# Sparse attention and a feed-forward layer in one kernel: seven instead of ten pairs of attention tiles ahead of the FFN, and the first group's sixteen f-tiles in one row

## The chip, the core and the metric

The kernel runs on one core of one Trainium2 chip. The metric is the device time of one execution in microseconds. Every duration and time of day below is in microseconds unless marked ns; times of day count from the start of the profiled span.

## The reference

Attention over 8 batches, 8 heads, 576 positions and 64 columns a head. Heads 0 to 3 have a local mask (a query sees the 32 positions that end at it), heads 4 to 7 a strided one (a query sees the earlier positions with the same remainder modulo 32). The result, 4608 tokens by 512, goes through a feed-forward layer of width 2048.

```
rel = pos[:, None] - pos[None, :]
mask_local = (rel >= 0) & (rel < 32)
mask_strided = (rel >= 0) & (pos[None, :] % 32 == pos[:, None] % 32)
scores = where(mask, scale * q @ k.T, -1e9)        # per batch and head
attn = exp(scores - max); attn /= sum(attn) + 1e-9
x = (attn @ v), heads side by side                 # 4608 x 512
h = x @ w_in                                       # 512 x 2048
g = h * sigmoid(1.702 * h)
out = g @ w_out                                    # 2048 x 512
```

## The kernel before, in words

**Attention.** Only the blocks that the masks leave are computed. A unit of work is a pair: two neighbouring tiles of queries for all four heads of one kind. A local tile has 96 queries and 128 keys. A strided tile holds the positions of 6 or 5 remainders, 18 positions each, so 108 or 90 queries and as many keys. A batch has three strided pairs (of 108, 90 and 90 rows) and three local pairs. There are 48 pairs. Of each, TensorE makes the scores (`s`, or `u` for odd pairs in the pipeline), VectorE the negated maximum (`nmax`), ScalarE eight exponentials with their sums, VectorE the reciprocals, GpSimd the multiplication by them (`pr`). Then `pr` is transposed into `pt_l` or `pt_s`, TensorE multiplies by v (`a`), ScalarE rounds the result to the upper part of x (`xhl`, `xhs`), and VectorE subtracts to get the lower part (`xll`, `xls`).

**Feed-forward.** The tokens are worked in twelve groups of 384, the width in sixteen f-tiles of 128. Every operand of a product is split in an upper and a lower part, and three products stand for one: `ffn1` (line 447) issues 12 products of 128 x 384 into `h`, `act` (line 461) makes tanh on ScalarE, `g` on VectorE, `gh` on ScalarE and `gl` on VectorE, and `ffn2` (line 480) issues 9 products of 128 x 512 into the three output banks `o` of the group. The main loop (line 599) runs over a list `steps` of (group, f-tile). Turn s issues `ffn1` of step s, `act` of step s - 1, work on pairs, and `ffn2` of step s - 2 (`LAG`).

**Weights.** w_in and w_out come as pairs of 32-bit words, 1 MB an f-tile, into tiles `raw` (`load_w`, line 336). `weights` (line 401) is a generator. Each of its beats, a unit, is one large ScalarE operation, followed one beat later by its VectorE operation: scale, then low with a join on VectorE (both on `raw`), then split (`w<-raw` on ScalarE, `w<-raw,w` on VectorE). So an f-tile takes three units, and split of f-tile f is unit 3f + 4. `raw` and the finished weights share 16 tiles, so the last f-tile is only loaded when the one ahead of it is finished. `weigh(n)` (line 440) runs the generator up to n units; one of a turn's units stands inside `act`, between tanh and `gh`.

**The order of the work.** `InOrder` (line 98) keeps TensorE's instructions in program order throughout, and those of VectorE, ScalarE, GpSimd and the DMA queue on SyncE as long as weights are still to be made (line 600). So the queues of these engines in that stretch are read off the program. Before the main loop stands a pipeline over the first `n0` pairs (lines 550 to 578). There the mask is added by a product on TensorE, and `pr` is transposed by TensorE (`turn_pr`, banks `t`). The later pairs stand in the main loop: `windows` lists those that belong to each next group, `due` gives the turn at which VectorE transposes a pair, `turn` the same the other way round, and `begins` the turn at which its scores are made. Values follow one turn after the transposes. The pair's exponentials are spread over the turns between (line 627).

In before, `n0` is 10: groups 0 and 1 have all their pairs in the pipeline. `spans` (line 527) puts the first eight f-tiles of group 0, then group 1 whole, then the second half of group 0. Weights are made at three units a turn for eight turns and at one and a half a turn after that (line 619). Group 0's first half is kept in SBUF (`halves`, line 501) and added at the end (line 510).

Of the kernel before, what the change touches and what calls it, by code (L numbers as in the profile page):

```python
# [18 lines left out]
P = 128  # L19
# [23 lines left out]
SOON = 11  # L43
LAG = 2
RAWB = 4
NH = NF // 2
WEIGHED = 7


def _pairs():  # L50

    def strided(b):
        return [("s", b, c) for c in range(0, len(RES), U)]

    def local(j):
        n = G // QL
        return [("l", i // NL, i % NL) for i in range(j * n, (j + 1) * n, U)]

    def weave(a, b):
        return [u for i in range(max(len(a), len(b))) for u in a[i : i + 1] + b[i : i + 1]]

    first = {}
    for b in range(B):
        first.setdefault(b * S // G, []).extend(strided(b))
    ahead = local(0) + first[0]
    windows = [weave(first.get(j + 1, []), local(j + 1)) for j in range(NG - 1)] + [[]]
    ahead += windows[0]
    windows[0] = []  # L70
    return ahead + [u for w in windows for u in w], windows, len(ahead)


# [1 line left out]
def attn_ffn(ctx, tc, qk, vs, w_in, w_out, masks, ident, out):  # L75
# [48 lines left out]
    def load_qk(p):  # L124
        if p < len(pairs) and p not in qks:
            qks[p] = st4([P, 2, 2, U, P], F32, f"qk_{p}")
            for g in (slice(0, 1), slice(1, 2)) if p == 0 else (slice(0, 2),):
                sync.dma_start(out=qks[p][:, :, g], in_=qk[p][:, :, g])
# [63 lines left out]
    def maxima(p):  # L192


        nq, nk, mask = geom(p)
        sps, pr, n = banks.pop(p), prs[p % AHEAD], mask.shape[1]
        nmax = nmaxs[p] = small.tile([P, HU], F32, tag="nmax", name=f"nmax_{p}")
        if p < n0:
            for j in range(2):
                vector.tensor_reduce(  # L200
                    out=nmax[:nq, j * 2 * U : (j + 1) * 2 * U],
                    in_=sps[j][:nq, : 2 * U * nk].rearrange("p (h n) -> p h n", n=nk),
                    axis=AX.X, op=ALU.max, negate=True,
                )
            vector.tensor_scalar_mul(out=nmax[:nq], in0=nmax[:nq], scalar1=SCALE)
            exps[p] = [
                (sps[i // (2 * U)][:nq, i % (2 * U) * nk : (i % (2 * U) + 1) * nk], SCALE)
                for i in range(HU)
            ]
            return  # L210
        for j in range(2):
            o = pr[:nq, j * 2 * U : (j + 1) * 2 * U, :nk]
            if n == 2:
                o = o.rearrange("p (g u) n -> p g (u n)", g=2)
            vector.scalar_tensor_tensor(
                out=o, in0=sps[j][:nq, : 2 * U * nk].rearrange("p (a n) -> p a n", a=n),
                scalar=SCALE, in1=mask, op0=ALU.mult, op1=ALU.add,
            )
        vector.tensor_reduce(
            out=nmax[:nq], in_=pr[:nq, :, :nk], axis=AX.X, op=ALU.max, negate=True  # L220
        )
        exps[p] = [(pr[:nq, i, :nk], 1.0) for i in range(HU)]
# [159 lines left out]
    def split_w(f):  # L382

        part = w_tile([P, 2, 2, DM], F32R, f"w_{f}")
        wih[f], wil[f] = (part[:, 0, i].rearrange("p (c n) -> p c n", c=NC) for i in range(2))
        woh[f], wol[f] = (part[:, 1, i] for i in range(2))
        vs = [(part[:, m, 0], part[:, m, 1], v) for m, v in words.pop(f)]

        def high():
            for hi, _, v in vs:  # L390
                scalar.copy(out=hi, in_=v)

        def low():
            for hi, lo, v in vs:
                vector.tensor_tensor(out=lo, in0=v, in1=hi.bitcast(F32), op=ALU.subtract)
            if f + RAWB < NF - 1:
                load_w(f + RAWB)

        return high, low
# [40 lines left out]
    def weigh(n):  # L440

        while made[0] < n and next(wgen, 0) is None:
            made[0] += 1
# [31 lines left out]

    outs = {}

    halves = {}

    def ffn2(j, f, i, parts):  # L480


        first = (0, NH) if j == 0 else (0,)
        last = (NH - 1, NF - 1) if j == 0 else (NF - 1,)
        if f in first and 0 in parts:
            outs[j, i] = bank(f"o_{j}_{i}")
        ps = outs[j, i]
        gh, gl = gs[j, f]
        tok = slice(i * P, (i + 1) * P)
        ws = ((gh, woh), (gh, wol), (gl, woh))  # L490
        for n in parts:
            g, w = ws[n]
            matmul(
                ps, lhsT=g[:, tok], rhs=w[f],
                start=(f in first and n == 0), stop=(f in last and n == 2),
            )
        if f not in last or 2 not in parts:
            return
        del outs[j, i]
        if f < NF - 1:  # L500
            o = halves[i] = const.tile([P, DM], F32, name=f"half_{i}")
            if i == 1:
                vector.tensor_scalar_mul(out=o, in0=ps, scalar1=0.5)
            else:
                scalar.mul(out=o, in_=ps, mul=0.5)
            return
        make = st4 if j == NG - 1 and i == 2 else st2
        o = make([P, DM], F32, f"out_{j}_{i}")
        if j == 0:
            vector.scalar_tensor_tensor(  # L510
                out=o, in0=ps, scalar=0.5, in1=halves[i], op0=ALU.mult, op1=ALU.add
            )
        elif i == 1:
            scalar.mul(out=o, in_=ps, mul=0.5)
        else:
            vector.tensor_scalar_mul(out=o, in0=ps, scalar1=0.5)
        r = j * G + i * P
        sync.dma_start(out=out[r : r + P, :], in_=o)
        if i == NT - 1:
            del xs["l", j], xs["s", j]  # L520
# [3 lines left out]
            next(gen, None)  # L524


    spans = [(0, 0, NH), (1, 0, NF), (0, NH, NF)] + [(j, 0, NF) for j in range(2, NG)]
    steps = [(j, f) for j, f0, f1 in spans for f in range(f0, f1)]
    load_qk(1)
    load_v(0)  # L530
    ident_sb = const.tile([P, P], F32, name="ident_sb")
# [8 lines left out]
    def scaled(p):  # L540
        run(halfway.pop(p))

    def late_part(p):
        run(valued.pop(p))
# [5 lines left out]
    for i in range(n0):  # L550
        if i + 1 < n0:
            scores(i + 1)
            load_qk(i + 3)
        if i >= 1:
            scaled(i - 1)
        if i >= 2:
            fetch_pt(i - 2)
        if i >= 3:
            late_part(i - 3)
        if i + 1 < n0:  # L560
            maxima(i + 1)
        halfway[i] = softmax(i)
        run(halfway[i], 4)
        if i >= 2:
            value_products(i - 2)
            load_v(i)
            run(valued[i - 2], 1)
        if i % 2 and i // 2 + 1 < RAWB:
            load_w(i // 2 + 1)
        weigh(i and i + 1)  # L570
        if i == n0 - 2:
            turn_pr(i - 1)
            ffn1(*steps[0], (0, 1))
        elif i == n0 - 1:
            ffn1(*steps[0], (2, 3))
            turn_pr(i - 1)
        elif i >= 1:
            turn_pr(i - 1)


    at = {}
    for n, (j, f) in enumerate(steps):
        at.setdefault(j, n)
    due = {}
    p = n0
    for j, w in enumerate(windows):
        if not w:
            continue
        end = at[j + 1]
        begin = end - NH + 1 if j == 1 else at[j]  # L590
        for i in range(len(w)):
            due[begin + i * (end - 1 - begin) // len(w)] = p
            p += 1

    late, turn = None, {p: s for s, p in due.items()}
    begins = {}
    for p in range(n0, len(pairs)):
        begins[max(turn.get(p - AHEAD, -1) + 1, turn[p] - SOON)] = p
    for s in range(len(steps) + LAG):
        strict[0] = made[0] < 3 * NF + 3  # L600
        cur = steps[s] if s < len(steps) else None
# [1 line left out]
        p, q, r = due.get(s), due.get(s - 1), begins.get(s)  # L603
        if cur:
            if s == 1:
                scaled(n0 - 1)
                fetch_pt(n0 - 2)
                late_part(n0 - 3)
            if s == 2:
                fetch_pt(n0 - 1)  # L610
                late_part(n0 - 2)
            if s > 0:
                ffn1(*cur, range(NC))
            if s in (1, 2):
                value_products(n0 - 3 + s)
            if s == 1:
                turn_pr(n0 - 1)
        if 0 < s <= len(steps):
            goal = WEIGHED + min(3 * (s + 1), 3 * NH + (s + 1 - NH) * 3 // 2)
            act(*steps[s - 1], lambda: weigh(min(made[0] + 1, goal)))  # L620
            if s in (1, 2):
                run(valued[n0 - 3 + s], 1)
            weigh(goal)
            if s == 2:
                late_part(n0 - 1)
        if late is not None:
            run(late[0], -(-4 // (late[1] - s)) if late[1] > s else HU)
        if p is not None:
# [96 lines left out]
```

## Time and profile before

| | |
|---|---|
| median of 3 runs | 940.06 us (939.3 to 940.83) |
| profiled execution | 941.84 us, its span 940.1 us, mean granted TensorE clock 0.998 |
| TensorE, VectorE, ScalarE, GpSimd busy | 98%, 55%, 43%, 9% of the span |
| `o` products (1728) | 44% of the chain that ended last |
| `h` products (2304) | 43% of that chain |
| bytes moved | 65.10 MB, mean 69 GB/s |

The page gives busy time by engine, the span in 40 slices, the chain of work that ended last and groups of instructions. A row of a timeline has the start, the time covered, the engine, the line (all instructions are recorded at line 108, the helper that issues them), the operation, output and inputs by name, the shapes and the count; in brackets stands the idle time before it and what ended it. A row of the chain has the start, the time and what it was. A row of windows has the stretch, then busy time of each engine, the granted clock, the share of the DMA engines and GB/s.

### The profile page before, as it was taken

To read this page: it belongs to the slowest core of one execution; us is meant where nothing else is said; L and a number is where in the kernel's file an instruction comes from. 1 tells how busy PE (TensorE), PEld (TensorE's weight loads), DVE (VectorE), ACT (ScalarE), POOL (GpSimd) and SP (SyncE) were. 2 spreads that over 40 slices of the span, in tenths; PEclk is the share of its full clock that TensorE was granted. 3 is DMA by queue.
4 is the path that set the end of the run, shared out by engine and by line. 5 is a ranking of instruction groups with operands and counts; after the bars stand their busy time and mean duration, and the time that the engine had idled before them with its cause. 6 is when DMAs were issued, how large, how long until landed. Compare 5 with 4: busy or idle time off the path is not lost.

```text
span 940.1 us, 14682 instructions
## 1 busy us (share of the span) xinstructions
PE 924.2 (98%) x5668; PEld 815.1 (87%) x5668; DVE 520.3 (55%) x999; ACT 408.0 (43%) x1289; POOL 85.7 (9%) x56
## 2 busy tenths in 40 slices
PE   7799999999999999999999999999999999999998
PEld 5589888888888888888888888898888888888997
DVE  4886564676666554626756665544756665422322
ACT  6997563434344443325343443333344444222221
POOL 3310000011001100101010100000010101000000
PEclk9999999999999999999999999999999999999999
DMA  8894020222121111103212121102211210000000
GB/s 269 307 336 172 1 90 29 73 68 68 48 77 59 54 36 66 35 1 102 60 42 81 54 69 45 36 22 68 65 37 56 80 46 12 34 1 1 34 1 33
DMA packets 24373, 65.10 MB, mean 69 GB/s; under 512 B 2672, under 2 KB 3440, under 8 KB 24304
## 3 DMA queue, kind: packets, MB, share of 16 engines
q1 hardware_dynamic: 24304, 64.17, 20.4%
q8 instruction: 44, 0.72, 0.3%
q14 instruction: 25, 0.20, 0.1%
HBM read 54.72 MB, written 9.44 MB: 68 GB/s over the span
## 4 chain that ended last, share of the span: by engine, by line
PE 95%; DVE 2%; DMA 1%; ACT 1%; issue 0%; POOL 0%; SPq 0%; ACTq 0%; POOLq 0%
PE o L108 44%; PE h L108 43%; PE s L108 4%; PE a L108 4%; DMA qk<-qk 1%; ACT pr L108 1%; PE u L108 1%; DVE nmax L108 0%; PE t L108 0%; DVE w L108 0%; DVE raw L108 0%; POOL pr L108 0%; DVE pt_l L108 0%; ACT raw L108 0%; SPq L108 0%
## 5 line engine op out<-in xcount | busy, mean ns | idle before, releaser
L108 PE MATMUL o<-w,gh 128*128 128x512 f32 x1152 | 307.8, 399 | 0.0
L108 PEld LDWEIGHTS o<-w,gh 128*128 128x128 f32 x1152 | 210.9, 188 | 40.0
L108 PE MATMUL h<-xhl,w 128*128 128x384 f32 x768 | 231.3, 342 | 0.4 <-DVE w L108 0.4
L108 PE MATMUL h<-xhs,w 128*128 128x384 f32 x768 | 226.3, 335 | 0.0
L108 DVE SCALAR_TENSOR_TENSOR g<-g,h 128x384 f32<-128x384 f32 x192 | 106.4, 554 | 195.8 <-ACT g L108 194.8
L108 ACT ACTIVATE g<-h 128x384 f32<-128x384 f32 x192 | 93.6, 488 | 246.2 <-PE h L108 178.6
L108 PE MATMUL o<-w,gl 128*128 128x512 f32 x576 | 169.4, 395 | 0.0
L108 DVE TENSOR_TENSOR gl<-g,gh 128x384 fp32r<-128x384 f32 x192 | 126.2, 657 | 73.5 <-ACT gh L108 72.3
L108 ACT ACTIVATE pr<-pr,nmax 96x128 f32<-96x128 f32 (+2 forms) x304 | 114.2, 378 | 113.1 <-DVE nmax L108 109.6
L108 ACT CAST gh<-g 128x384 fp32r<-128x384 f32 x192 | 99.0, 516 | 130.2 <-DVE g L108 129.9
L108 PEld LDWEIGHTS h<-xhl,w 128*128 128x128 f32 x768 | 141.5, 188 | 9.4 <-DVE w L108 0.7
L108 POOL TENSOR_TENSOR pr<-pr,rinv 96x1024 f32<-96x1024 f32 (+2 forms) x48 | 82.1, 1710 | 708.0 <-DVE rinv L108 631.5
L108 PEld LDWEIGHTS h<-xhs,w 128*128 128x128 f32 x768 | 141.5, 188 | 0.1
L108 PEld LDWEIGHTS o<-w,gl 128*128 128x128 f32 x576 | 108.2, 188 | 26.0
L108 PE MATMUL h<-xll,w 128*128 128x384 f32 x384 | 129.7, 338 | 0.0
L108 PE MATMUL h<-xls,w 128*128 128x384 f32 x384 | 128.3, 334 | 0.0
L108 PEld LDWEIGHTS h<-xll,w 128*128 128x128 f32 x384 | 72.1, 188 | 8.5
L108 PEld LDWEIGHTS h<-xls,w 128*128 128x128 f32 x384 | 72.1, 188 | 0.0
L108 DVE TENSOR_SCALAR rinv<-ssum 96x8 f32<-96x8 f32 (+2 forms) x48 | 8.0, 167 | 93.9 <-ACT pr L108 93.8
L108 ACT ACTIVATION_READ_ACCUMULATOR pr<-pr,nmax 96x1 f32 (+2 forms) x304 | 57.1, 188 | 0.0
L108 DVE STREAM_TRANSPOSE pt_l<-pr 32x256 f32<-32x256 f32 x120 | 52.1, 434 | 3.7 <-POOL pr L108 2.3
L108 PE MATMUL s<-qk 64*96 64x128 f32 (+2 forms) x688 | 46.2, 274 | 1.7 <-DMA qk<-qk 1.7
(52 smaller groups left out, 543.2 us busy)
## 6 DMA issues: line engine op xcount, KB each, us to landing
qk<-qk SPq DMA_DIRECT2D x47, 512.0 KB, 4.2
v<-vs SPq DMA_DIRECT2D x48, 256.0 KB, 2.9
out<-out SPq DMA_DIRECT2D x36, 256.0 KB, 2.5
raw<-w_in SPq DMA_DIRECT2D x16, 512.0 KB, 5.4
raw<-w_out SPq DMA_DIRECT2D x16, 512.0 KB, 6.2
qk<-qk SPq DMA_DIRECT2D x2, 256.0 KB, 4.0
masks_sb<-masks SPq DMA_DIRECT2D x1, 128.0 KB, 2.1
ident_sb<-ident SPq DMA_DIRECT2D x1, 64.0 KB, 5.5
```

What stands on the lines that cost most here:

```text
L108: ins = call(*args, **kw)
```

## The change

The pipeline ahead of the FFN holds seven pairs: the five of group 0 and group 1's two local ones. Group 1's three strided pairs become a window of group 0, due at turns 6, 9 and 12, with their scores at turns 3, 7 and 10. The steps run group by group, sixteen f-tiles each, and the half sums go. The goal of units at turn s is 6 + 3(s + 1) up to turn 2 and 8 + 3(s + 1) after. In the pipeline, w_1 is loaded one iteration sooner and the loads of w_2 to w_4 are placed by hand; part of the first products moves past the end of the pipeline. Group 2's two local pairs, the first of the later windows, become due at turns 18 and 24 in place of 25 and 28. The negated maximum of pair 0 is scaled by halves, and the last output tile is evicted by ScalarE and VectorE together.

```diff
-NH = NF // 2
-WEIGHED = 7
+NEARLY = 5
+WEIGHED = 6, 8
...
-    ahead += windows[0]
-    windows[0] = []
+    ahead += windows[0][1::2]
+    del windows[0][1::2]
...
             for j in range(2):
+                heads = slice(j * 2 * U, (j + 1) * 2 * U)
...
-            vector.tensor_scalar_mul(out=nmax[:nq], in0=nmax[:nq], scalar1=SCALE)
+                if p and j == 0:
+                    continue
+                x = nmax[:nq, heads if p == 0 else slice(0, HU)]
+                vector.tensor_scalar_mul(out=x, in0=x, scalar1=SCALE)
...
-            if f + RAWB < NF - 1:
+            if NEARLY <= f + RAWB < NF - 1:
                 load_w(f + RAWB)
...
-        first = (0, NH) if j == 0 else (0,)
-        last = (NH - 1, NF - 1) if j == 0 else (NF - 1,)
-        if f in first and 0 in parts:
+        if f == 0 and 0 in parts:
...
-        if f < NF - 1:
-            o = halves[i] = const.tile([P, DM], F32, name=f"half_{i}")
...
-        if j == 0:
-            vector.scalar_tensor_tensor(
-                out=o, in0=ps, scalar=0.5, in1=halves[i], op0=ALU.mult, op1=ALU.add
-            )
-        elif i == 1:
+        if i == 1:
             scalar.mul(out=o, in_=ps, mul=0.5)
+        elif j == NG - 1 and i == NT - 1:
+            n = DM // 2
+            scalar.mul(out=o[:, n:], in_=ps[:, n:], mul=0.5)
+            vector.tensor_scalar_mul(out=o[:, :n], in0=ps[:, :n], scalar1=0.5)
...
-    spans = [(0, 0, NH), (1, 0, NF), (0, NH, NF)] + [(j, 0, NF) for j in range(2, NG)]
-    steps = [(j, f) for j, f0, f1 in spans for f in range(f0, f1)]
+    steps = [(j, f) for j in range(NG) for f in range(NF)]
...
-            load_qk(i + 3)
+            if i + 3 < n0:
+                load_qk(i + 3)
...
-        if i % 2 and i // 2 + 1 < RAWB:
-            load_w(i // 2 + 1)
+        if i in (0, 3, 5, 6):
+            load_w((0, 3, 5, 6).index(i) + 1)
         weigh(i and i + 1)
+        if i >= 1:
+            turn_pr(i - 1)
         if i == n0 - 2:
-            turn_pr(i - 1)
             ffn1(*steps[0], (0, 1))
-        elif i == n0 - 1:
-            ffn1(*steps[0], (2, 3))
-            turn_pr(i - 1)
...
-        begin = end - NH + 1 if j == 1 else at[j]
+        begin = 6 if j == 0 else (j * NF + 2 if j == 1 else j * NF)
         for i in range(len(w)):
-            due[begin + i * (end - 1 - begin) // len(w)] = p
+            due[begin + i * (j * NF + NF - 1 - begin) // len(w)] = p
             p += 1
...
-    for p in range(n0, len(pairs)):
-        begins[max(turn.get(p - AHEAD, -1) + 1, turn[p] - SOON)] = p
+    begins = {turn.get(p - 1, 2) + 1: p for p in range(n0, n0 + 5)}
+    for p in range(n0 + 5, len(pairs)):
+        begins[max(turn[p - AHEAD] + 1, turn[p] - SOON)] = p
...
             if s == 1:
+                load_qk(n0)
                 scaled(n0 - 1)
                 fetch_pt(n0 - 2)
                 late_part(n0 - 3)
+                ffn1(*steps[0], (2, 3))
+                value_products(n0 - 2)
+                turn_pr(n0 - 1)
+                weigh(9)
...
-            if s in (1, 2):
-                value_products(n0 - 3 + s)
-            if s == 1:
-                turn_pr(n0 - 1)
+            if s == 2:
+                value_products(n0 - 1)
         if 0 < s <= len(steps):
-            goal = WEIGHED + min(3 * (s + 1), 3 * NH + (s + 1 - NH) * 3 // 2)
+            goal = WEIGHED[s > 2] + 3 * (s + 1)
             act(*steps[s - 1], lambda: weigh(min(made[0] + 1, goal)))
...
             if s == 2:
                 late_part(n0 - 1)
+                load_v(n0)
```

More of the change, by code (lines that the diff above doesn't have):

```diff
@@ L199, in maxima @@
             for j in range(2):
+                heads = slice(j * 2 * U, (j + 1) * 2 * U)
                 vector.tensor_reduce(
-                    out=nmax[:nq, j * 2 * U : (j + 1) * 2 * U],
+                    out=nmax[:nq, heads],
                     in_=sps[j][:nq, : 2 * U * nk].rearrange("p (h n) -> p h n", n=nk),
@@ L476, in attn_ffn @@
     outs = {}
-    halves = {}
     def ffn2(j, f, i, parts):
-        first = (0, NH) if j == 0 else (0,)
-        last = (NH - 1, NF - 1) if j == 0 else (NF - 1,)
-        if f in first and 0 in parts:
+        if f == 0 and 0 in parts:
             outs[j, i] = bank(f"o_{j}_{i}")
@@ L494, in ffn2 @@
                 ps, lhsT=g[:, tok], rhs=w[f],
-                start=(f in first and n == 0), stop=(f in last and n == 2),
+                start=(f == 0 and n == 0), stop=(f == NF - 1 and n == 2),
             )
-        if f not in last or 2 not in parts:
+        if f < NF - 1 or 2 not in parts:
             return
         del outs[j, i]
-        if f < NF - 1:
-            o = halves[i] = const.tile([P, DM], F32, name=f"half_{i}")
[L502 to L506, printed above, removed]
         make = st4 if j == NG - 1 and i == 2 else st2
         o = make([P, DM], F32, f"out_{j}_{i}")
-        if j == 0:
-            vector.scalar_tensor_tensor(
-                out=o, in0=ps, scalar=0.5, in1=halves[i], op0=ALU.mult, op1=ALU.add
-            )
-        elif i == 1:
+        if i == 1:
             scalar.mul(out=o, in_=ps, mul=0.5)
+        elif j == NG - 1 and i == NT - 1:
+            n = DM // 2
+            scalar.mul(out=o[:, n:], in_=ps[:, n:], mul=0.5)
+            vector.tensor_scalar_mul(out=o[:, :n], in0=ps[:, :n], scalar1=0.5)
         else:
@@ L567, in attn_ffn @@
             run(valued[i - 2], 1)
-        if i % 2 and i // 2 + 1 < RAWB:
-            load_w(i // 2 + 1)
+        if i in (0, 3, 5, 6):
+            load_w((0, 3, 5, 6).index(i) + 1)
         weigh(i and i + 1)
+        if i >= 1:
+            turn_pr(i - 1)
         if i == n0 - 2:
-            turn_pr(i - 1)
             ffn1(*steps[0], (0, 1))
-        elif i == n0 - 1:
-            ffn1(*steps[0], (2, 3))
-            turn_pr(i - 1)
[L577 to L583, printed above, removed]
     due = {}
@@ L586, in attn_ffn @@
     for j, w in enumerate(windows):
-        if not w:
-            continue
-        end = at[j + 1]
-        begin = end - NH + 1 if j == 1 else at[j]
+        begin = 6 if j == 0 else (j * NF + 2 if j == 1 else j * NF)
         for i in range(len(w)):
-            due[begin + i * (end - 1 - begin) // len(w)] = p
+            due[begin + i * (j * NF + NF - 1 - begin) // len(w)] = p
             p += 1
     late, turn = None, {p: s for s, p in due.items()}
-    begins = {}
-    for p in range(n0, len(pairs)):
-        begins[max(turn.get(p - AHEAD, -1) + 1, turn[p] - SOON)] = p
+    assert len(set(turn.values())) == len(turn)
+    begins = {turn.get(p - 1, 2) + 1: p for p in range(n0, n0 + 5)}
+    for p in range(n0 + 5, len(pairs)):
+        begins[max(turn[p - AHEAD] + 1, turn[p] - SOON)] = p
+    assert len(begins) == len(turn)
     for s in range(len(steps) + LAG):
```

## The prediction

> **What bounds the kernel now.** I read the page first, then the chain of waits, then the timelines of ScalarE (ACT), VectorE (DVE) and the DMA queue over the first 250 us. All times are in us, durations are from the one profiled execution.
>
> ```profile
> PE 924.2 (98%) x5668; PEld 815.1 (87%) x5668; DVE 520.3 (55%) x999; ACT 408.0 (43%) x1289; POOL 85.7 (9%) x56
> ```
>
> TensorE carries the span. The shares hide that the first 90 us are another regime, which is the one that changes. The chain shows it; I number a step of the FFN by its place s in the list of steps (0 first), and read off where the `o` products of a turn of the loop end.
>
> ```profile
> 59.20 2.30 PE o L108 x9
> 61.50 2.11 PE h L108 x12
> 63.62 2.10 PE o L108 x9
> ...
> 115.34 2.10 PE o L108 x9
> ```
>
> These are turns 2, 3 and 15: they end at 61.5, 65.7 and 117.4. A turn takes 4.21 without a gap (12 `h` in 2.11, 9 `o` in 2.10), so turns 6, 9 and 12 end at 78.3, 91.0 and 103.6; the 1.2 over that up to 117.4 are a local pair's scores in turn 14. But look at ScalarE in the same stretch:
>
> ```profile
> 61.72 0.50 ACT L108 ACTIVATE g<-h 128x384 f32<-128x384 f32 x1
> 62.09 1.15 ACT L108 CAST w<-raw 128x1024 fp32r<-128x1024 f32 x1
> 63.11 0.55 ACT L108 CAST gh<-g 128x384 fp32r<-128x384 f32 x1
> 63.53 2.21 ACT L108 ACTIVATE raw<-raw 128x1024 f32<-128x1024 f32 x2
> 65.64 0.48 ACT L108 ACTIVATE g<-h 128x384 f32<-128x384 f32 x1
> ```
>
> From one tanh to the next it works 3.92 without a pause: tanh 0.37, three units of weight conversion (1.02 for the cast, 2.1 for the pair on `raw`), 0.42 for `gh`. While one f-tile of weights is converted per turn, ScalarE has 0.29 to spare beside TensorE's 4.21, and that is all.
>
> **The change, part by part.**
>
> *Three pairs leave the pipeline.* Pairs 0 to 6 keep their places there (only 5 becomes a local pair). In before, the exponentials of pair 6 begin at 34.60. The load of w_1 is asked for one iteration sooner, which removes the 0.67 in the second row, so they begin at 33.9.
>
> ```profile
> 21.62 1.17 ACT L108 ACTIVATE raw<-raw 128x1024 f32<-128x1024 f32 x1 [0.67 <-DMA raw<-w_out]
> ...
> 34.60 0.41 ACT L108 ACTIVATE pr<-s,nmax 96x128 f32<-96x128 f32 x1
> ```
> ```profile
> 54.00 0.88 PE L108 MATMUL a<-pt_l,v 128*64 128x96 f32 x16
> ```
>
> (The split maximum of pair 0 frees ScalarE 0.7 sooner, but pair 1's exponentials wait for pair 1's own maximum: nothing.) Behind 33.9, in ScalarE's queue up to split_w(2): 8 exponentials with their read-outs (0.34 each), a copy of x (0.4), five units (5.2), tanh, `gh` and another copy (1.2): 43.4. VectorE's low half of w_2 follows (1.13 and 0.3 in the queue): 44.8. Ten of the twelve `h` of step 2 wait for it (1.7), then the value products (0.88): the first `o` at 47.4 and the end of turn 2 at 49.5, **12.0 ahead** of 61.5.
>
> *The three pairs come back beside the FFN.* What one costs TensorE there, from strided pairs of later windows:
>
> ```profile
> 225.52 0.77 PE a L108 x16
> 226.29 0.81 PE s L108 x16
> 227.09 2.30 PE o L108 x9
> ...
> 240.73 0.94 PE s L108 x16
> ...
> 273.33 0.89 PE a L108 x16
> ```
>
> One pair of 108 rows (0.89 + 0.94) and two of 90 (0.77 + 0.81): 5.0, and 0.2 for an `o` behind such work, in three turns more: **5.6**. The same pairs on the other engines:
>
> ```profile
> 207.79 2.23 DVE L108 STREAM_TRANSPOSE pt_s<-pr 32x256 f32<-32x256 f32 x5
> ...
> 229.26 0.90 DVE L108 TENSOR_REDUCE nmax<-pr 90x8 f32<-90x720 f32 x1
> ```
> ```profile
> 202.56 0.36 ACT L108 ACTIVATE pr<-pr,nmax 90x90 f32<-90x90 f32 x1
> ...
> 202.92 0.35 ACT L108 ACTIVATE pr<-pr,nmax 90x90 f32<-90x90 f32 x1
> ```
>
> ScalarE: 8 x 0.355 + 0.42 for the copies of x = 3.3 a pair. VectorE: the reduction 0.9, about as much for adding the mask to the same 720 elements, 5 transposes 2.2 (7 for 108 rows, 3.1), and with the low halves (next fence) and the reciprocal 4.9. GpSimd's three multiplications fall where it is idle. On SP's queue the pairs' loads now stand between the weight loads: load_v(7) waits for pair 5's value products (40.6), load_qk(9) for pair 7's scores (52.7); the f-tiles behind them (8 and 12) are converted from 65 and 89 on. Nothing waits there.
>
> *Sixteen f-tiles in a row.* Before, only eight are converted at one per turn; the others at half of that. Now all are, and the pairs are due at turns 6, 9 and 12. A cycle of three turns: ScalarE 3 x 3.92 + 3.3 = 15.1; TensorE 3 x 4.21 + 1.58 + 0.2 = 14.4; VectorE per turn
>
> ```profile
> 61.10 0.59 DVE L108 TENSOR_TENSOR xls<-a,xhs 128x120 fp32r<-128x120 f32 x2
> 62.25 0.56 DVE L108 SCALAR_TENSOR_TENSOR g<-g,h 128x384 f32<-128x384 f32 x1 [0.56 <-ACT g L108]
> 62.73 1.22 DVE L108 SCALAR_TENSOR_TENSOR raw<-raw 128x1024 uint32<-128x1024 uint32 x1
> 63.86 0.55 DVE L108 TENSOR_TENSOR gl<-g,gh 128x384 fp32r<-128x384 f32 x1
> 64.33 1.22 DVE L108 TENSOR_TENSOR w<-raw,w 128x1024 fp32r<-128x1024 f32 x1
> ```
>
> 3.2 by the distances, so 9.6 + 4.9 = 14.5. Three engines at 14.4 to 15.1, each in program order. So I walk the queues turn by turn: an operation starts when its engine is free and its inputs are there (0.05 later).
>
> - Turn 3: the goal jumps by two units, 6.0 for ScalarE instead of 3.92. Then it stops at pair 7's exponentials: its scores are done at 52.7, but VectorE is in `w` and `raw` until 56.0 and needs 2.15 for mask and maximum (ScalarE free at 55.8, starts at 58.2). Two exponentials there, four in turn 4, two in turn 5: its tanh is reached at 58.9, 64.3, 68.9, 72.8. The weights of steps 5, 6 and 7 come 0.4 to 0.7 late. Turns 3 to 6 end at 70.2, where before has 78.3: 3.9 of the lead lost (1.1 of it pair 7's scores).
> - Turns 7 to 9: `transpose` of pair 7 stands on VectorE (73.0 to 76.1) ahead of turn 7's `g`. ScalarE gets to `gh` at 74.3 and waits 2.35 for it. TensorE reaches pair 7's value products at 72.7 and waits **3.4** for the transposes. Only behind them come pair 8's scores, and behind `w`, `gl`, `raw` and `xls` VectorE's mask and maximum: ScalarE waits 2.4 again at pair 8's first exponential. 15.1 + 2.35 + 2.4 makes its cycle 19.7. TensorE: 76.1 + 0.89 + 0.81 + 2.3 + 2 x 4.21 = 88.5; before 91.0.
> - Turns 10 to 12 alike with five transposes: TensorE waits 1.1 and 0.7 for w_10, then 2.6 for pair 8's transposes, and ends turn 12 at 107.3; before 103.6.
> - Turns 13 to 15: w_15 has a slot only when w_14 is finished (VectorE, 112.7).
>
> ```profile
> 125.11 1.22 DVE L108 TENSOR_TENSOR w<-raw,w 128x1024 fp32r<-128x1024 f32 x1
> ```
> ```profile
> 126.40 0.33 SPq L108 DMA_DIRECT2D raw<-w_in  x1
> ```
> ```profile
> raw<-w_out SPq DMA_DIRECT2D x1, 512.0 KB, 4.4
> ```
>
> The load is issued as w_14 ends (126.33 in before); its second half goes out 0.4 later and lands 4.4 after that, 5.0 in all: here at 117.7. ScalarE comes to it at 112.0: 5.8 of waiting that before hides under half-rate turns. Two units, join and split: 122.5. VectorE's low half of w_15 is emitted one turn on, behind pair 10's first exponentials (126.0, waiting for its maximum) and the next tanh: 128.9. TensorE, held 1.8 by w_13 and 3.7 by pair 9's transposes, stands at step 15 from 123.2; 1.7 of `h` and 2.1 of `o` end turn 15 at 132.7. Before: 117.4.
>
> From 12.0 ahead to **15.3 behind**: 27.3 lost, 5.6 as work, 21.7 as waits. Turns 16 to 31 hold the same work in both (two local pairs), from 32 the plans are the same; TensorE has no reserve there to win anything back.
>
> *Small parts.* The half sums and their additions lie on engines with room: nothing. The last output tile is now evicted by two engines:
>
> ```profile
> 936.40 0.69 DVE L108 TENSOR_SCALAR out<-o 128x512 f32<-128x512 f32 x1 [0.71 <-PE o L108]
> ```
>
> Half of 0.69 less: -0.3. The clock:
>
> ```profile
> 42.00:43.00 1.00, 0.00 (x0) 0.00 (x0) 0.96 (x5) 1.00 (x3) 0.42 (x1) 1.00 1.06 426
> ...
> 44.00:45.00 1.00, 1.00 (x16) 0.93 (x14) 0.00 (x0) 1.00 (x8) 0.00 (x0) 0.50 0.42 162
> ```
>
> After TensorE's idle stretch around 42 the granted clock is 0.50 (the third figure from the right), for some 3 us. Waits of 2.6 and more can bring that back: from 0 (the engine has slack after most of them) to 6 (four times 1.5); I take **1.0**, near the low end, since ScalarE sets the pace there. The Trainium skill ("TensorE: Matmul & The Clock Gate", "Why this matters for your kernels") says to avoid idle gaps over some 3 us, since an idle window halves the clock. In this trace a shorter gap was enough; by that rule the waits under 3 us would cost no clock, and the term would be about 0.6.
>
> **Sum.** 15.3 - 0.3 + 1.0 = 16.0. The profiled execution took 941.84 (span 940.1), so it would be 957.8; on the median of 940.06 the forecast is **956.0**. Slower.
>
> **The rivals.**
>
> 1. *The queues absorb the waits* (faster). By sums alone 15.1 against 14.4 leaves ScalarE only 0.7 short per cycle, and TensorE starts 12.0 ahead. If the late turns cost nothing but the work: 940.06 - 12.0 + 5.6 - 0.3 = 933.4. It decides as soon as all of TensorE's waits in turns 3 to 15 stay under 4.5. For it: in turns 3 to 8 before, ScalarE is full and TensorE never waits. Against: there no pair stands in the same queues. The Trainium skill ("Perfetto Trace Analysis", "Optimization Strategy") speaks for this rival: where a kernel has several regimes, interleaving them may help. No run so far shows it at full conversion rate. 0.15.
> 2. *Half of the waits.* The transposes or the maxima fit into other gaps than I placed them: 956.0 - 11 = 945. 0.17.
> 3. *The clock drops at each long wait*: the upper bound of 6 instead of 1.0: 961. 0.10.
> 4. *It does not start sooner*: the pipeline waits for data instead, as it may have around 42 in the rows of the clock (DMA share 1.06 while TensorE stands). Now fewer loads stand in that stage, so at most 3 of the lead is gone: 959. 0.05.
> 5. Losses cancel the lead: 940. 0.05.
>
> **How the numbers follow.** My forecast has 0.48 (950 to 960); the predicted time is its time. Slower: 0.48 + 0.17 + 0.10 + 0.05 = 0.80; faster 0.15; within 0.2% (1.9 us, about what a measurement of this kernel can tell from no change) 0.05. The range leaves out rival 1 and a few per cent above: 940 to 964. Without rivals 1 and 5 it would be 943 to 964.
>
> **What would show it.** In the profile after: the first `o` of the chain near 47; the end of turn 15 near 133; ScalarE above 9 tenths from 10 to 115; in the chain of waits DVE `pt_s` and `w` ahead of PE `a` and `h`, and the wait for raw_15 (ACT `t` on DMA) near 5. Turns 3 to 15 in rows of 4.21 with only `s` and `a` between would prove me wrong (rival 1); a first `o` after 52 would point to rival 4.

## The result, and the profile after

| | before | after |
|---|---|---|
| median of 4 runs each | 939.68 us (939.05 to 940.83) | 962.71 us (961.83 to 963.9) |
| profiled execution, its span | 941.84, 940.1 | 961.83, 959.9 |
| mean granted TensorE clock | 0.998 | 0.988 |

Ratio 1.0237, 95% interval 1.0221 to 1.0253: 23 us slower by the medians, 22.3 by the ratio. The forecast of 956.0 had the sign and the mechanism, and its range (940 to 964) holds the time, with 1.3 to spare. The time itself came out 6.7 above the forecast, and the narrower 950 to 960, to which I gave 0.48, doesn't hold it. By the spans of the two profiled executions the loss is 19.8: the one of before was 2.2 above its median, the one of after 0.9 below its own.

All instructions of after are recorded at line 110. The page's shares by engine:

```profile
PE 929.9 (97%) x5638; PEld 817.6 (85%) x5638; DVE 532.3 (55%) x1009; ACT 410.3 (43%) x1289; POOL 85.5 (9%) x56
...
L110 PE MATMUL h<-xhl,w 128*128 128x384 f32 x768 | 232.2, 343 | 11.0 <-DVE w L110 11.0
```

The same group before:

```profile
L108 PE MATMUL h<-xhl,w 128*128 128x384 f32 x768 | 231.3, 342 | 0.4 <-DVE w L108 0.4
```

TensorE's busy time is up by only 5.7, though there are fewer matmuls, and the shares look as before. The group row says more: ahead of these `h` products TensorE stood idle 11.0 for VectorE's low halves of the weights, before 0.4. The place is in TensorE's timeline (start, time, instruction, in brackets the idle time before it and what ended it):

```profile
48.00 1.67 PE L110 MATMUL o<-w,gh 128*128 128x512 f32 x6
...
50.21 0.34 PE L110 MATMUL h<-xhl,w 128*128 128x384 f32 x1
...
71.38 0.34 PE L110 MATMUL h<-xhl,w 128*128 128x384 f32 x1
...
77.94 1.71 PE L110 MATMUL a<-pt_s,v 108*64 108x108 f32 x16 [2.62 <-DVE pt_s L110]
...
84.59 0.33 PE L110 MATMUL h<-xhl,w 128*128 128x384 f32 x1
...
93.00 0.34 PE L110 MATMUL h<-xhl,w 128*128 128x384 f32 x1
...
97.92 0.84 PE L110 MATMUL a<-pt_s,v 90*64 90x90 f32 x16 [1.74 <-DVE pt_s L110]
...
110.99 0.34 PE L110 MATMUL h<-xhl,w 128*128 128x384 f32 x1
...
114.05 0.61 PE L110 MATMUL h<-xhl,w 128*128 128x384 f32 x2 [2.54 <-DVE w L110]
...
119.52 1.47 PE L110 MATMUL a<-pt_s,v 90*64 90x90 f32 x16 [2.52 <-DVE pt_s L110]
```

And the chain that ended last, from step 15's low half of the weights on:

```profile
117.78 4.49 DMA raw<-w_out
...
132.40 0.61 DVE w L110
133.05 2.04 PE h L110 x10
135.09 2.10 PE o L110 x9
137.19 2.11 PE h L110 x12
```

The first `o` is at 48.00 (before 59.20 by the chain, 59.13 by the timeline). The first `h` product of the turn behind shows that turn 2 ends at 50.21, turn 6 at 71.38, turn 9 at 93.00 and turn 12 at 110.99, and by the chain turn 15 ends at 137.19. Before has 61.5, 78.3, 91.0, 103.6 and 117.4. The timeline's row of an `h` starts some 0.17 ahead of the chain's (turn 15 ends at 137.02 by the timeline). By timelines alone TensorE is 11.1 ahead at the end of turn 2 (50.21 for 61.34) and 19.7 behind at the end of turn 15 (137.02 for 117.28); by the chains it is 19.8 behind there, and 19.8 is the difference of the spans: behind turn 15 nothing is lost or won.

The waits of the stretch 45 to 145, by engine, summed (total, times, longest):

```profile
ACT pr L110 <- DVE nmax L110: 10.8, 4, 3.2
PE h L110 <- DVE w L110: 9.9, 8, 2.5
ACT gh L110 <- DVE g L110: 8.7, 5, 3.2
...
PE a L110 <- DVE pt_s L110: 6.9, 3, 2.6
...
ACT t L110 <- DMA raw<-w_in: 4.1, 1, 4.1
```

TensorE waits 16.8 for VectorE. ScalarE waits 19.5 for VectorE in the two rows shown, 27.5 in all its rows on VectorE, and 4.1 for the first half of the last f-tile's load. No engine is full: between 60 and 140 each of the three has gaps. The row of after, then that of before:

```profile
60.00:140.00 80.00, 63.45 (x345) 53.77 (x344) 58.91 (x92) 52.71 (x121) 6.31 (x4) 0.89 0.27 96
```
```profile
60.00:140.00 80.00, 80.00 (x420) 71.64 (x419) 53.45 (x77) 55.93 (x100) 1.90 (x1) 1.00 0.33 124
```

In these 80 us TensorE is busy 63.45 (the first figure behind the comma), VectorE 58.91 (the third), ScalarE 52.71 (the fourth). Before, TensorE is busy for all 80 of them.

The chain of after has no piece of TensorE between 62.68 and 133.05: in that stretch it runs through ScalarE and VectorE alone, and through the load at 117.78. By it, TensorE's waits and slow stretches there follow from these two engines and don't set the end.

### The profile page after: what moved, and what is told of

It is laid out like the page before. It is cut to its first block, busy times and chain, and to the rows that moved or that the text cites. A ratio compares the mean times of both kernels' runs of the same rounds, so it can differ in the third digit from the quotient of the medians.

```text
span 959.9 us, 14612 instructions
## 1 busy us (share of the span) xinstructions
PE 929.9 (97%) x5638; PEld 817.6 (85%) x5638; DVE 532.3 (55%) x1009; ACT 410.3 (43%) x1289; POOL 85.5 (9%) x56
## 3 DMA queue, kind: packets, MB, share of 16 engines
q1 hardware_dynamic: 24304, 64.17, 19.5%
## 4 chain that ended last, share of the span: by engine, by line
PE 88%; ACT 4%; DVE 3%; DMA 2%; issue 1%; SPq 0%; POOL 0%; ACTq 0%; POOLq 0%
PE o L110 40%; PE h L110 40%; PE s L110 4%; PE a L110 4%; ACT pr L110 2%; DMA qk<-qk 1%; ACT w L110 1%; ACT raw L110 1%; DVE w L110 1%; PE u L110 1%; PE t L110 0%; DVE nmax L110 0%; DMA raw<-w_out 0%; DVE pt_s L110 0%; ACT gh L110 0%
## 5 line engine op out<-in xcount | busy, mean ns | idle before, releaser
L110 ACT ACTIVATE pr<-pr,nmax 96x128 f32<-96x128 f32 (+2 forms) x328 | 122.8, 376 | 112.0 <-DVE nmax L110 112.0
L110 ACT ACTIVATION_READ_ACCUMULATOR pr<-pr,nmax 96x1 f32 (+2 forms) x328 | 61.5, 187 | 0.0
L110 DVE STREAM_TRANSPOSE pt_s<-pr 32x256 f32<-32x256 f32 x119 | 51.6, 433 | 1.8 <-POOL pr L110 0.4
```

Source lines behind the costliest of these rows:

```text
L110: ins = call(*args, **kw)
```

## The experiments

The theories. **A**, mine: three strided pairs' work stands in VectorE's and ScalarE's queues, in program order, between the operations that make the weights; each engine waits in turn for another that is held by something else. **B**: the sixteen f-tiles in a row, at three units of weights a turn, are the cost by themselves. **C**: ScalarE's sum, 15.1 a cycle, sets the pace, and nothing else matters. Times are medians; the kernel before had 941.43 beside the first four kernels and 941.19 beside the last four, where after, by its ratio, would be at 963.7 and 963.5. A difference of two ratios below carries about 2 us of uncertainty.

**The row of sixteen with ten pairs in the pipeline** (against before)

```diff
-    spans = [(0, 0, NH), (1, 0, NF), (0, NH, NF)] + [(j, 0, NF) for j in range(2, NG)]
+    spans = [(j, 0, NF) for j in range(NG)]
...
-            goal = WEIGHED + min(3 * (s + 1), 3 * NH + (s + 1 - NH) * 3 // 2)
+            goal = WEIGHED + 3 * (s + 1)
```

with `first = (0,)`, `last = (NF - 1,)`, and no half sums.

> The kernel before with one part of the change alone: group 0's sixteen f-tiles in a row, no half sums, three units of weights in every turn; the ten pairs stay in the pipeline. Theory A (the waits come from three strided pairs standing in the same in-order queues as the full-rate weights): without the pairs ScalarE has 3.92 us of work per turn of 4.21 and only the last f-tile's chain can show, so 2 us over before, 942 us (938 to 946). Rival B (sixteen f-tiles in a row are the cost, the pairs only move it): most of the 23 us, 955 or more.

Measured: 942.89, ratio 1.0018 (1.0008 to 1.0028). In its timeline TensorE waits for weights twice between 57 and 140, 0.40 at 57.47 and 1.51 for the last f-tile, which must wait for a slot here too:

```profile
116.15 0.62 PE L108 MATMUL h<-xhl,w 128*128 128x384 f32 x2 [1.51 <-DVE w L108]
```

B falls as the main cause: at the full rate for all sixteen, with no pair in the same queues, TensorE waits 1.9 and the kernel loses 0.18%, under 2 us. TensorE doesn't start early here; the run without the softmax below has the early start too. Splitting group 0 in halves, as before does, is worth no more than that.

**The first two exponentials a turn later** (against after, no work left out)

```diff
             late = softmax(r), turn[r]
-            run(late[0], 1)
+            if r >= n0 + 4:
+                run(late[0], 1)
```

> The kernel after, with no work moved between engines: the first two exponentials of pairs 7 to 10 are no longer issued in the turn of their scores, right behind the maximum, but with the others in the next turns. Theory A: ScalarE's four waits of 2.5 to 3.2 us for the maximum go, and of the 11 us some 4.5 reach the end: 958 us (955 to 960). Rival C (ScalarE simply has more work than the turns hold; the order does not matter): 962.7, no change within 1 us.

Measured: 959.34, ratio 1.0192 (1.0177 to 1.0207), some 4 below after. The waits of 45 to 145:

```profile
ACT gh L110 <- DVE g L110: 16.6, 10, 3.6
...
PE a L110 <- DVE pt_s L110: 9.9, 3, 4.6
...
PE h L110 <- DVE w L110: 4.7, 5, 2.1
...
ACT pr L110 <- DVE nmax L110: 2.8, 1, 2.8
```

No work went, only its place in one queue changed, and the time moved: the order counts, as A says. But not by as much as the wait that it was aimed at: ScalarE waits 8.0 less for the maximum and 7.9 more for `g` (8.7 to 16.6), and TensorE 5.2 less for weights and 3.0 more for the transposes (6.9 to 9.9).

**No multiplication on GpSimd for the three pairs** (against after; their probabilities stay unnormalised)

```diff
+        if n0 <= p < n0 + 3:
+            return
         gpsimd.tensor_tensor(
```

> The kernel after without GpSimd's multiplication by the reciprocals for pairs 7 to 9; their rows stay unnormalized. In the trace of after three w subtractions of VectorE that lie beside that multiplication took 2.45, 2.20 and 2.19 us in place of 1.22. If it is the multiplication that slows them: 1.22 again, and 2 to 3 us less, 960 us. If the slow rows have another reason (the queue, a wait counted as work): they stay, and the time stays at 962.7. Rival C expects no change, since ScalarE's work is the same.

Measured: 961.17, ratio 1.0210 (1.0194 to 1.0225), 2.5 below after, about the uncertainty. What it was made for is in VectorE's timeline. After, in turns 6 and 8:

```profile
70.79 2.45 DVE L110 TENSOR_TENSOR w<-raw,w 128x1024 fp32r<-128x1024 f32 x1
...
74.76 3.12 DVE L110 STREAM_TRANSPOSE pt_s<-pr 32x256 f32<-32x256 f32 x7
...
91.92 2.20 DVE L110 TENSOR_TENSOR w<-raw,w 128x1024 fp32r<-128x1024 f32 x1
```

GpSimd's timeline in after:

```profile
70.53 1.63 POOL L110 TENSOR_TENSOR pr<-pr,rinv 108x864 f32<-108x864 f32 x1 [31.72 <-DVE rinv L110]
91.64 1.40 POOL L110 TENSOR_TENSOR pr<-pr,rinv 90x720 f32<-90x720 f32 x1 [19.49 <-DVE rinv L110]
```

And VectorE's in this experiment:

```profile
71.53 1.22 DVE L110 TENSOR_TENSOR w<-raw,w 128x1024 fp32r<-128x1024 f32 x1
...
91.85 1.22 DVE L110 TENSOR_TENSOR w<-raw,w 128x1024 fp32r<-128x1024 f32 x1
```

Beside the multiplication the subtraction takes 2.45 and 2.20, without it 1.22. That GpSimd slows VectorE is shown; that it is worth 2.5 us is only likely. The profiled executions agree with it: from the end of TensorE's wait for step 3's weights to the end of its wait for step 15's it is 79.74 here (51.63 to 131.37) and 82.10 in after (50.95 to 133.05), 2.4 less. This execution gave part of that back, as its clock was halved behind the last wait:

```profile
131.37 2.35 PE h L110 x10
133.72 3.33 PE o L110 x9
```

In after the same products took 2.04 and 2.10.

**No last f-tile of weights** (against after; step 15 multiplies by the weights of step 14)

```diff
-                load_w(NF - 1)
-                order += words(NF - 1)
-                for _ in range(2):
+                for t in (wih, wil, woh, wol):
+                    t[NF - 1] = t[f]
+                for _ in range(6):
                     yield
-        later()
-        yield
+                return
```

> The kernel after without the load and conversion of the sixteenth f-tile; its products use the weights of the fifteenth. Takes away the chain from w_14 over the load to w_15 that ends turn 15. Theory A: turns 13 to 15 shrink by some 4 to 5 us, 958 us; the waits at the transposes and at w_13 stay. If that chain alone had made the last part of the loss: 10 us less, 953. Rival C (amount of ScalarE work, 3.1 us of which go): 959.5.

Measured: 959.29, ratio 1.0196 (1.0179 to 1.0213), 3.9 below after. The load, its conversion and the 4.1 that ScalarE waits for it cost about 4 together, not more: TensorE's wait for the transposes of pair 9 (at 120.15) grew from 2.52 to 3.46 in its place.

**No softmax for the three pairs** (against after; mask, maximum, exponentials, reciprocals, multiplication and transposes left out, TensorE's scores and values kept)

```diff
+        if p < n0 + 3:
+            exps[p] = []
+            return
...
+        if n0 <= p < n0 + 3:
+            yield from (None,) * 4
+            return
...
-        for qb in range(-(-nq // BL)):
+        for qb in range(0 if n0 <= p < n0 + 3 else -(-nq // BL)):
```

> The kernel after without what the three strided pairs 7 to 9 cost VectorE, ScalarE and GpSimd in their softmax: no mask addition, maximum, exponentials, reciprocals, multiplication and transposes for them; scores and value products on TensorE stay, with stale data in front of the values, and so do their 5.6 us. Theory A (the waits come from these pairs' work in the queues of the weights): turn 15 ends near 117 as in before, 943 us (940 to 947). If the row of sixteen f-tiles with an early start were too fast for the weights by itself: still 950 or more.

Measured: 944.37, ratio 1.0033 (1.0022 to 1.0045). 19 of the 22 us are gone. In TensorE's timeline between 50 and 140 two waits are left (turn 2 ends at 51.85):

```profile
52.57 0.62 PE L110 MATMUL h<-xhl,w 128*128 128x384 f32 x2 [0.21 <-DVE w L110]
...
114.42 1.01 PE L110 MATMUL h<-xhl,w 128*128 128x384 f32 x2 [4.28 <-DVE w L110]
```

Its chain from there:

```profile
114.42 3.57 PE h L110 x10
117.99 3.25 PE o L110 x9
```

That the loss needs the pairs' work on the other engines, and not the weights alone, is shown. And even without that work the change doesn't win: 4.28 for the last f-tile, TensorE's own work for the pairs and the clock behind the wait (10 `h` in 3.57 for 2.03, 9 `o` in 3.25 for 2.10) eat the lead. That much of B is left when the row of sixteen starts early.

**Without the exponentials alone** (against after; 24 of them left out, the reciprocals taken of the maxima)

```diff
-            scalar.activation(
+            if not n0 <= p < n0 + 3:
+              scalar.activation(
...
+        x = nmax if n0 <= p < n0 + 3 else ssum
```

> The kernel after without the 24 exponentials of pairs 7 to 9 on ScalarE (8.5 us of its work; the reciprocals are taken of the maxima in place of the sums); all else stays. It brings ScalarE's sum for three turns from 15.1 to 12.3 us, under TensorE's 14.4. Rival C (the sum of ScalarE's work sets the pace): TensorE sets it again, nearly all of the 21 us of waits go, 943. Theory A (the order couples the engines; VectorE's maxima and transposes stay in front of g and w): 8 us less than after, 955 (952 to 957).

Measured: 951.92, ratio 1.0114 (1.0099 to 1.0129), 11.6 below after. ScalarE has 12.3 of work a cycle here against TensorE's 14.4; by C the loss should be gone, and half of it is there. It was 0.1 beyond the range that I gave A: ScalarE's share is larger than I put it. The waits of 45 to 145:

```profile
ACT gh L110 <- DVE g L110: 14.7, 10, 3.2
...
PE a L110 <- DVE pt_s L110: 6.2, 3, 3.4
...
PE h L110 <- DVE w L110: 4.0, 4, 3.3
```

ScalarE now waits more (14.7 for `g`) and TensorE still stands 10.2 for VectorE.

**Without the transposes alone** (against after; 17 left out, so the three pairs' values are made of old contents of `pt_s`)

```diff
-        for qb in range(-(-nq // BL)):
+        for qb in range(0 if n0 <= p < n0 + 3 else -(-nq // BL)):
```

> The kernel after without VectorE's 17 transposes of pairs 7 to 9 (7.4 us of its work; the value products read stale data). Theory A: ScalarE's waits for g behind the transposes go, and TensorE's three waits for pt_s; the maxima and the chain to w_15 stay: 4 to 5 us less than after, 958 (955 to 960). Rival C: VectorE's work does not matter, 962.7.

Measured: 959.88, ratio 1.0197 (1.0180 to 1.0214), 3.8 below after. The wait they cause (6.9 of TensorE) is gone from its list; what stands in its place:

```profile
PE h L110 <- DVE w L110: 12.6, 7, 4.3
...
PE h L110 <- DVE xls L110: 2.4, 1, 2.4
PE o L110 <- ACT gh L110: 1.0, 1, 1.0
...
ACT gh L110 <- DVE g L110: 4.5, 4, 2.6
```

2.7 of it went over to the wait for weights (9.9 in after), and 2.4 and 1.0 to two waits that after doesn't have. So TensorE stands idle 16.0 in place of 16.8, hardly less; what got shorter is the path through ScalarE and VectorE: the weights of step 15 let TensorE go on at 129.13 and not at 133.05. ScalarE's wait for `g`, which stood behind the transposes, is half as long.

Added up, the multiplication (2.5), the exponentials (11.6) and the transposes (3.8) make 17.9 of the 19.2 that the whole softmax costs. With some 2 us of uncertainty on each it isn't shown that the prices add; the 1.3 that remain for mask, maximum and reciprocals, which weren't taken out alone, can't be told from nothing.

**Ten pairs, with the earlier loads and the split last eviction** (against before; meant to beat both)

```diff
-            if f + RAWB < NF - 1:
+            if NEARLY <= f + RAWB < NF - 1:
...
-        if i % 2 and i // 2 + 1 < RAWB:
-            load_w(i // 2 + 1)
+        if i in (0, 3, 6, 8):
+            load_w((0, 3, 6, 8).index(i) + 1)
```

with `NEARLY = 5` and the eviction of the last output tile as in after.

> A version meant to beat both: the kernel before with ten pairs and half sums, and three things of the change or like it: w_1 is loaded one iteration sooner, w_3 and w_4 one and three iterations later (behind the last pairs' q and k, which came late around 42 us in before), and the last output tile is evicted by two engines. If the wait for pair 9's q and k and the halved clock after it cost what the trace shows, 1.8 us and 1.5 us: 2 to 3.5 us less than before, 937.5. If the pipeline is held by ScalarE alone: 0.3 less for the eviction, 940.

Measured: 940.59, ratio 0.9992 (0.9982 to 1.0002): no gain that can be told, so the 2 to 3.5 that I expected are out. Its first `o` is at 56.85, 2.35 sooner than in before's profile, and the two profiled spans differ by 1.8 (938.3 and 940.1); but before's profiled execution was 2.2 above its median, and the medians differ by 0.6. The gain of one profile isn't one of the kernel. The wait of `u` for `qk` that before has there (1.76 at 43.63) is gone. But in TensorE's timeline another stands two operations on:

```profile
45.87 0.84 PE L109 MATMUL a<-pt_s,v 90*64 90x90 f32 x16 [1.69 <-DVE xll L109]
```

No version was found that beats before.

## Why the prediction was right, and where its size was off

*The lead.* Predicted: first `o` at 47.4, 12.0 ahead at the end of turn 2. Measured 48.00 and 11.1. Right in size, so rival 4 (no sooner start) falls. The path to it was another than I wrote: VectorE's low half of w_2 was done at 44.90 (I had 44.8), and TensorE, which I had waiting for it, came to it only at 45.36, held up by its own work since 38.00, with the clock at 0.50 up to 43. That the two met within 0.5 is luck. Six of the experiments hold the same program up to TensorE's wait for step 3's weights, which ends at 50.95 in after; in their profiles it ends 0.1 to 1.6 later. So the turn ends of a single profile are uncertain by as much.

*The pairs' work on TensorE*, 5.6. The run without the softmax shows it nearly bare. It ends turn 2 at 51.85, 9.5 ahead of 61.34, and its span of 944.0 is 3.9 longer than before's: 13.4 lost, of which 4.5 are waits and 2.7 the clock (1.54 and 1.15 in the rows above). 6.2 remain, near 5.6.

*One price that I had at nothing.* "GpSimd's three multiplications fall where it is idle" was true and not enough: it looked at GpSimd alone. The trace of before showed the effect already, on the smaller subtraction `gl`, and I read past it. GpSimd's and VectorE's timelines of before:

```profile
187.96 1.90 POOL L108 TENSOR_TENSOR pr<-pr,rinv 96x1024 f32<-96x1024 f32 x1 [12.20 <-DVE rinv L108]
```
```profile
188.90 1.38 DVE L108 TENSOR_TENSOR gl<-g,gh 128x384 fp32r<-128x384 f32 x1 [0.58 <-ACT gh L108]
```

`gl` alone takes 0.55, beside the multiplication 1.38. In after it hits the weights' subtraction three times: 1.2, 1.0 and 1.0 more.

*Turns 3 to 6*: predicted end 70.2, measured 71.38, of which 0.7 was there at the end of turn 2. ScalarE began pair 7's exponentials at 59.10, where I had 58.2.

*Turns 7 to 9*: predicted 18.3, measured 21.6. The order of events is the one I wrote: pair 7's transposes stand ahead of `g`, ScalarE waits for `g` (3.17; predicted 2.35), TensorE for the transposes (2.62; predicted 3.4), then ScalarE for pair 8's maximum (2.61; predicted 2.4). ScalarE's timeline:

```profile
78.51 0.51 ACT L110 CAST gh<-g 128x384 fp32r<-128x384 f32 x1 [3.17 <-DVE g L110]
...
84.19 0.37 ACT L110 ACTIVATE pr<-pr,nmax 90x90 f32<-90x90 f32 x1 [2.61 <-DVE nmax L110]
```

But the value products start at 77.94, where I had 76.1: 1.84 late. Pair 7's late exponentials (0.9) and the subtraction beside GpSimd's multiplication (1.2) make that up, less 0.3. Then TensorE runs at half the clock:

```profile
80.00:84.00 4.00, 4.00 (x23) 3.26 (x20) 3.65 (x7) 1.58 (x4) 0.00 (x0) 0.50 0.00 0
```

The granted clock (third figure from the right) is 0.50 from 78 to about 84, and values, scores and `o` take 6.65 (77.94 to 84.59) in place of my 0.89 + 0.81 + 2.30 = 4.00. 1.84 + 2.65 is the 4.5 by which turn 9 ended later than predicted (93.00 for 88.5). The Trainium skill ("TensorE: Matmul & The Clock Gate", "Why this matters for your kernels") names idle gaps over about 3 us as the ones to avoid. Here 2.62, with 1.40 a few us ahead of it, was enough.

The 2.65 don't reach the end. TensorE's next wait ends at 94.18, 0.06 behind VectorE's subtraction for step 10 (91.92 to 94.12), and the chain ahead of that subtraction, back to 62.68, holds nothing of TensorE's. At full clock TensorE would have stood there 3.3 in place of 0.66. The second drop (114 to 126) is taken up in the same way by the 2.29 at 133.05. So the 1.0 that I set aside for the clock was not needed in these turns, and the reason that I gave for the low end, that ScalarE sets the pace there, holds for both, with VectorE beside ScalarE. No run takes the clock out alone; this is read from the chain.

**The step that was mis-sized is GpSimd's term, at nothing.** All three slow subtractions stand in the chain that ended last. It counts the rest of the first two, up to the `gl` behind them, as issue:

```profile
70.79 1.02 DVE w L110
...
91.92 1.02 DVE w L110
...
111.88 2.12 DVE w L110
```

Together they put up to 3.2 on it, and the late start of pair 7's exponentials 0.9. w_14 was finished at 117.34, where I had 112.7: 4.6 late. The rest stays open; a small part of it is my sum for ScalarE's cycle, 15.1 + 2.35 + 2.4, which is 19.85 and not 19.7. The run without GpSimd's multiplications got 2.5 back, with some 2 us of uncertainty, so it bears out that this term reaches the end, but not its size to the us.

*Turns 10 to 12*: predicted 18.8, measured 18.0. *Turns 13 to 15*: predicted 25.4, measured 26.0. Both near. ScalarE's wait for the load of w_15 was 4.06, and 0.8 for its second half, and not 5.8: the load was issued at 117.4 and not at 112.7, as w_14 was finished later, and ScalarE came to it at 116.8 and not at 112.0. Behind the wait ten `h` took 2.04, where I had 1.7.

*Sum.* 15.3 behind by the prediction, 19.8 measured: 4.5 more. With the 1.0 that I had set aside for the clock and the -0.3 that is 3.8 on the spans, and 4.0 on the profiled execution's time (961.83 for 957.8). The other 2.7 up to the 6.7 of the medians are 1.8 that I took off for before's median and 0.9 by which after's median is above its profiled run. Beside the span 23.0 stands for the medians: 3.0 of the 3.2 between them is the choice of runs that were profiled (2.2 and 0.9). Of the -0.3 for the split eviction nothing can be seen.

*The rivals.* That the queues absorb the waits (933.4) and that the losses cancel (940) are out by 20 us and more. Half of the waits (945) is out too: TensorE waited 16.8 in the stretch, against 21.7 in my walk, and the two drops of the clock stand where it would else have waited longer. The clock rival (961) was nearest in time, by luck: the clock did drop, but the chain shows neither drop as a cost to the end. The Trainium skill ("Perfetto Trace Analysis", "Optimization Strategy") holds that interleaving regimes may improve a kernel with several; in these runs it cost 23 us, and the softmax that was interleaved carries 19 of them.

*One sign that failed.* I expected ScalarE above 9 tenths from 10 to 115. It is busy 85.63 of these 105 us, and 49.42 of the 65 from 50 on. The sign didn't fit my own walk, in which ScalarE waits 4.75 of a cycle of some 19.8.

*Still open*: how the wait for maxima, for `g` and for transposes share the 19; each was moved or removed alone, and part of it came back at another. Another order of VectorE's queue within a turn (transposes behind `g`) wasn't tried.

## What to carry to other kernels

When work is moved beside a stage in which several engines are near full and each works in program order, don't compare sums of work: walk the queues operation by operation, since sums of 14.4 to 15.1 an engine gave three cycles of 21.6, 18.0 and 26.0 here. Where a term ended up is read off the chain that ended last, and not off the engine that is watched: at turn 9 TensorE was 4.5 later than I had walked, and 2.65 of that never reached the end. So count a halved clock of TensorE only where no later wait takes it up, as behind the last one (2.7 without the softmax, 1.5 without GpSimd's multiplications). Look in the trace for one engine's operations that get longer beside another's, also where the other one has time to spare.

## What the runs showed of the hardware

- A VectorE subtraction of two tensors hardly gets on while GpSimd's multiplication runs. In after the multiplications end at 72.16 and 93.04 and the subtractions at 73.24 and 94.12: 1.08 behind both times, against 1.22 for the whole subtraction alone. In before `gl` ends at 190.28, 0.42 behind the multiplication (189.86), against 0.55 alone. The Trainium skill ("SBUF — State Buffer", "SBUF: two separate sides") says just that: VectorE with two SBUF inputs and GpSimd share a pair of ports, and the one that starts first holds it for its whole instruction. Both traces agree.
- Short idle stretches of TensorE were followed by half the clock: 2.62 in after, and 1.69 in the last experiment, where the clock two us on is 0.50:

```profile
48.00:50.00 2.00, 2.00 (x12) 1.91 (x11) 1.10 (x4) 2.00 (x4) 1.39 (x1) 0.50 1.00 373
```

  But not each of them: in after the clock stayed at 1.00 behind the idle 1.74 that ended at 97.92 and the 2.29 that ended at 133.05. The same wait of 1.74 in the run without the last f-tile (to 98.53) was followed by 0.50 from 101 to 103. So the length of one gap doesn't decide, and what does stays open here. A drop at this place may be why removing the wait of 1.76 brought nothing that the medians show; it wasn't tried by itself.
